# Block attention, then a mixture of experts: P·V of the split units in two passes, row sums on VectorE and GpSimd, Q loaded twice

## The chip, the cores and the metric

One core of a Trainium2 chip. The metric is the device time of one execution in microseconds; the kernel before takes 961.75 us, the median of 3 runs (961.17 to 962.17).

## The reference

Attention over 4 batches, 8 heads, 576 tokens, head size 64, with a mask by blocks of 64 (a query sees its own block of keys and all earlier ones), then four experts on all 2304 tokens, weighted by normalised probabilities. All in float32.

```python
scores = scale * np.matmul(q, k.transpose(0, 1, 3, 2))
scores = np.where(block_i >= block_j, scores, -1000000000.0)
scores = scores - np.max(scores, axis=-1, keepdims=True)
attn = np.exp(scores)
attn = attn / (np.sum(attn, axis=-1, keepdims=True) + 1e-09)
x = np.matmul(attn, v)          # then to 2304 x 512
...
for e in range(E):
    h = np.maximum(x @ w1[e], 0.0)
    out += p[:, e:e + 1] * (h @ w2[e])
```

## The kernel before, in words

**Tokens and blocks.** `BLOCKS` cuts the tokens into five: one of 256 (the first 64 tokens of each batch) and four of 512 (the other 512 of one batch each). For each block the experts run in 32 chunks (4 experts times 8 slices of 128 hidden units), 160 chunks in all. `mm1` (L915) makes h of a chunk by 12 products, `mm2` (L960) adds the chunk to the four accumulators in PSUM by 12 more (6 in the first block). Each float32 operand is split into a high and a low part in fp32r (`w1h`, `w1l`, `xh`, `xl`, `hh`, `hl`), and a product takes three passes: high by high, high by low, low by high. A weight slice comes in by DMA (`w1r`, `w2r`), is cast (`a_copy`, L319, on ScalarE or VectorE) and subtracted (`tt`, L326, on VectorE).

**Attention.** Attention for block p is computed while the experts work on block p-1, in units of two heads (`unit`): four units for each 512-token block, sixteen in all. The first four (batch 0, `plain`) multiply in float32. The other twelve are split units, done while blocks 1 to 3 (163 to 779 us) go through the experts: Q and K are split in high and low. K's two parts are stacked on the 128 partitions (`KK`), and Q stands on both halves (`HH` high, `LL` low), so that a score product takes two passes, HH and LL (L517, L518). `q_thread` loads Q to the lower 64 partitions and copies it to the upper ones by a second DMA (`qr<-qr`). The scores stand transposed: keys on partitions, queries along the free dimension, in five pieces of 512, 448, 320, 192 and 64 queries (`pieces_of`) in the tile `S`. GpSimd takes the maximum over keys with a reduction over all partitions (L612), VectorE subtracts it, ScalarE takes the exponential (L630, L637).

**P·V before.** `NARROW` = 192: pieces wider than 192 are split in `PH` and `PL`, the others go as float32 in `PJ`. `VS` holds V high beside ones, and V low beside zeros, for both heads; `VJ` holds V in float32 beside ones. `pv_flow` (L689) makes a head's output in one PSUM bank: PH by V high, PH by V low, PJ by V, PL by V high. The 64 columns of ones make the row sums in the other half of the bank. `sums` reads them out with 1e-9 added (L698), the outputs go to `xs`, and the sums are turned (L713), inverted, turned back and multiplied.

**What sets the order.** `Flow.run` is a planner: every operation is a thread's next step, with engine, cost, inputs and buffers; at each turn the operation that can start earliest on its engine is written out next (`est`). So a change of costs, of inputs or of a delay in `est` changes the order in which all engines' instructions stand. Each engine then works through its own queue in that order, and waits where an input is late. `est` also keeps GpSimd's work and VectorE's SBUF work apart (`port`). DMAs are issued by SyncE, in one queue.

Of the kernel before, what the change touches and what calls it, by code (L numbers as in the profile page):

```python
# [17 lines left out]
PEO = 13.5  # L18


NARROW = 192
# [13 lines left out]
STEPS = [(0, 0, 2), (1, 0, 2), (0, 2, 4), (1, 2, 4)]  # L35

# [21 lines left out]
class Op:  # L58
    __slots__ = ("eng", "cost", "fn", "r", "u", "prio", "val", "port", "pen", "bytes")

    def __init__(self, eng, cost, fn, r, u, prio):
        self.eng, self.cost, self.fn, self.r, self.u, self.prio = eng, cost, fn, r, u, prio
        self.val = Val()
        self.port = False
        self.bytes = 0
        self.pen = lambda: 0.0


class Flow:
# [34 lines left out]
    def est(self, op):  # L104
        best = None
        for eng, cost in (op.eng if isinstance(op.eng, list) else [(op.eng, op.cost)]):
            t = self.clock[eng]
            for v in op.r:
                if v.t is None:
                    return None  # L110
                x = v.t + (self.SELF if v.eng == eng else self.LAT + (self.SLACK if eng == "pe" else 0.0))
                if x > t:
                    t = x
            for b in op.u:
                if b.base + self.LAT > t:
                    t = b.base + self.LAT
# [87 lines left out]
def kernel(  # L204
# [40 lines left out]
    MAXN = max(pieces_of(j[1], j[2])[1] - sum(x) for j, x in zip(every, wide_of))  # L245
# [30 lines left out]
    bufs("PJ", 2, [P, MAXN])  # L276
# [31 lines left out]
    def op(eng, cost, fn, r=(), u=(), prio=0.0):  # L308
        p = prio if callable(prio) else (lambda: prio)
        return Op(eng, cost, fn, r, u, p)  # L310

# [51 lines left out]
    def unit(u, ua, us, ju, pu, ph, job, dst, c):  # L363
# [47 lines left out]
        def q_thread():  # L411
# [4 lines left out]
            for h in range(2):  # L416
                for j in range(2):
                    p0, c0 = (64 * h + 32 * j, 0) if plain else (32 * j, h * W)
                    vals.append((yield dma(
                        qr.tile[p0:p0 + 32, c0:c0 + W].rearrange("c (i r) -> c i r", r=32),  # L420
                        q[b, h0 + h, q0:q1, 32 * j:32 * j + 32].rearrange("(i c) r -> c i r", c=32),
                        W * 128, u=[qr], prio=pr)))
            if not plain:
                vals = [(yield dma(qr.tile[64:128, :2 * W], qr.tile[0:64, :2 * W], W * 512, vals, [qr], prio=pr))]
# [16 lines left out]
        def v_thread():  # L441
# [47 lines left out]
        def s_thread():  # L489
# [6 lines left out]
            KK, ka, kb = st["k"]  # L496
            if plain:
# [22 lines left out]
            for h, ps_list in banks:  # L520
# [4 lines left out]
                if h is None:  # L525
# [13 lines left out]
                    m = yield op("pe", 220.0, fn, need(None), use, pr)  # L539
# [3 lines left out]
                else:  # L543
                    at = 0
                    corners = []
                    for j, a, w, _ in ps_list:
# [4 lines left out]
                        m = yield op("pe", cost(w), fn, need(h), use, pr)  # L551
# [51 lines left out]
        def m_thread():  # L603
# [22 lines left out]
            def exp_head(h):  # L626
                PH = PL = PJ = a = l = e = None
                if wide:
                    e = yield op("act", 0.833 * ce + 95,
                                 lambda _: nc.scalar.activation(Sv[:, h, :ce], Sv[:, h, :ce], AF.Exp, scale=scale), subs, [Sb], pr)  # L630
                if plain:
                    j = yield op("act", 0.833 * C + 95, lambda _: nc.scalar.activation(
                        Sv[:, h, :C], Sv[:, h, :C], AF.Exp, scale=scale), subs, [Sb], pr)
                    PJ = Sb
                elif narrow:
                    PJ = yield fl.take("PJ", ju + h)
                    j = yield op("act", 0.833 * (C - ce) + 95, lambda _: nc.scalar.activation(  # L637
                        PJ.tile[:, :C - ce], Sv[:, h, ce:C], AF.Exp, scale=scale), subs, [Sb, PJ], pr)
                if wide:
                    PH = yield fl.take("PH", pu + h)  # L640
                    a = yield a_copy(PH.tile[:, :ce], Sv[:, h, :ce], ce, [e], [Sb, PH], pr)
                    PL = yield fl.take("PL", pu + h)
                    l = yield tt("dve", PL.tile[:, :ce], Sv[:, h, :ce], PH.tile[:, :ce], SUB, ce, [e, a], [Sb, PH, PL], pr)
                st["P"][h] = (PH, PL, a, l, PJ, j)

            for h in range(2):
                yield from exp_head(h)
            if not plain:
                fl.give(Sb)
# [16 lines left out]

    def pv_flow(st, q0, dst, c, W, wide, narrow, C, plain, pr, bank_tag):
# [5 lines left out]
        for h in range(2):  # L673
# [5 lines left out]
            for x, g, dep in ((PH, 0, a), (PH, 3, a), (PJ, None, pj), (PL, 0, l)):  # L679
                for j, _a, w, c0 in narrow if g is None else wide:  # L680
                    if g is not None:
                        lhsT, cost, dv, c1 = VS.tile[:, j, h + g:h + g + 2, :], w / 2.4 + PEO, vv, c0
                    else:
                        lhsT = VJ.tile[:, j - narrow[0][0], h:h + 2, :] if j is not None else VJ.tile[:, VJ.tile.shape[1] - 1, 1 - h:3 - h, :]
                        cost, dv, c1 = 2 * max(107.0, 2 * w / 2.4 + 2.5), jv, h * C + c0 if plain else c0 - narrow[0][3]
                    todo.append((lhsT, x.tile[:, c1:c1 + w], w, cost, dv + [dep]))
            for i, (lhsT, rhs, w, cost, dep) in enumerate(todo):
# [3 lines left out]
                m = yield op("pe", max(107.0, cost), fn, dep, [pb] + [x for x in (VS, VJ, PH, PL, PJ) if x], pr)  # L691
            if not plain:
                fl.give(*[x for x in (PH, PL, PJ) if x])
            hi, lo = slice(64 * h, 64 * h + 64), slice(64 - 64 * h, 128 - 64 * h)
# [10 lines left out]
        if plain:  # L705
# [382 lines left out]
```

## Time and profile before

| | |
|---|---|
| median of 3 runs | 961.75 us |
| profiled execution | 961.83 us |
| its span, first to last instruction | 959.7 us |
| granted TensorE clock, mean | 0.998 |
| TensorE, VectorE, ScalarE, GpSimd busy | 99%, 72%, 43%, 6% |
| instructions | 12822 |
| DMA | 107.84 MB, mean 112 GB/s |

The busy share of TensorE counts its matmuls' whole durations, and these overlap: a 512-column product lasts about 390 ns, but the next one starts some 227 ns later. What a product costs is therefore read from start to start. VectorE's instructions overlap a little too. The share in idle time of an engine that nothing waits for costs nothing.

### The profile page before, as it was taken

How to read it: one execution, taken by the hardware profiler on the slowest of the kernel's cores; microseconds unless marked ns; L12 is line 12 of the kernel's file. 1: busy time of each engine (PE TensorE's matmuls, PEld its weight loads, DVE VectorE, ACT ScalarE, POOL GpSimd, SP SyncE). 2: the span in 40 equal slices, each digit the busy share in tenths (PEclk: the TensorE clock that was granted, in tenths of full speed). 3: DMA queues.
4: the chain of work that ended last, by engine and by line, in shares of the span. 5: the costliest groups of instructions: out<-in, count | busy, mean ns of one | idle time of the engine just before them, and what ended most of it. 6: DMA issues, size and time to landing. Idle time of an engine off the chain costs nothing.

```text
span 959.7 us, 12822 instructions
## 1 busy us (share of the span) xinstructions
PE 949.4 (99%) x4454; PEld 778.6 (81%) x4454; DVE 692.6 (72%) x1267; ACT 411.2 (43%) x734; POOL 58.2 (6%) x39
## 2 busy tenths in 40 slices
PE   8999998999999999999999999999999999999998
PEld 4777787888888888888888888888888888888886
DVE  6788877899787768888687679887877454545452
ACT  3575654555454424644544245453544222222221
POOL 2111010100101001010101001101010000000000
PEclk9999999999999999999999999999999999999999
DMA  9754446544252353525253355333423343333321
GB/s 168 172 143 133 113 147 165 148 116 112 77 124 83 100 139 103 150 69 140 78 120 86 92 137 139 108 96 109 113 88 88 100 142 99 99 92 98 97 66 44
DMA packets 211648, 107.84 MB, mean 112 GB/s; under 512 B 106112, under 2 KB 188032, under 8 KB 211584
## 3 DMA queue, kind: packets, MB, share of 16 engines
q1 hardware_dynamic: 208416, 106.24, 41.6%
q10 hardware_dynamic: 3168, 0.79, 0.5%
q8 instruction: 35, 0.57, 0.3%
q14 instruction: 29, 0.24, 0.1%
HBM read 99.13 MB, written 4.72 MB: 108 GB/s over the span
## 4 chain that ended last, share of the span: by engine, by line
PE 91%; DVE 5%; issue 1%; SPq 1%; POOL 1%; DMA 0%; ACT 0%; DVEq 0%; POOLq 0%
PE h L915 39%; PE acc L960 38%; PE att L689 7%; PE att L518 2%; PE att L517 2%; PE acc L689 1%; PE acc L505 1%; PE att L505 1%; DVE o L989 1%; SPq L313 1%; DVE w2l L326 1%; DVE qT L428 1%; DVE LL L326 1%; DVE KK L326 0%; DMA qr<-qr 0%
## 5 line engine op out<-in xcount | busy, mean ns | idle before, releaser
L915 PE MATMUL h<-xh,w1h 128*128 128x512 f32 (+1 forms) x640 | 238.7, 373 | 0.0
L915 PE MATMUL h<-xh,w1l 128*128 128x512 f32 (+1 forms) x640 | 236.2, 369 | 0.0
L915 PE MATMUL h<-xl,w1h 128*128 128x512 f32 (+1 forms) x640 | 236.1, 369 | 0.0
L960 PE MATMUL acc<-w2h,hh 128*128 128x512 f32 x576 | 225.3, 391 | 0.0
L960 PE MATMUL acc<-w2l,hh 128*128 128x512 f32 x576 | 224.6, 390 | 0.0
L960 PE MATMUL acc<-w2h,hl 128*128 128x512 f32 x576 | 224.4, 390 | 0.0
L319 ACT CAST w2h<-w2r 128x512 fp32r<-128x512 f32 x157 | 97.7, 622 | 194.1 <-PE acc L960 184.5
L932 ACT ACTIVATE hh<-h 128x512 fp32r<-128x512 f32 (+1 forms) x160 | 89.0, 556 | 210.5 <-PE h L915 205.0
L326 DVE TENSOR_TENSOR w2l<-w2r,w2h 128x512 fp32r<-128x512 f32 x160 | 111.4, 696 | 92.5 <-ACT w2h L319 91.5
L915 PEld LDWEIGHTS h<-xh,w1h 128*128 128x128 f32 x640 | 120.8, 189 | 25.1 <-issue 5.5
L915 PEld LDWEIGHTS h<-xh,w1l 128*128 128x128 f32 x640 | 120.7, 189 | 20.4
L915 PEld LDWEIGHTS h<-xl,w1h 128*128 128x128 f32 x640 | 120.8, 189 | 19.6 <-DVE xl L326 0.2
L960 PEld LDWEIGHTS acc<-w2h,hl 128*128 128x128 f32 x576 | 108.1, 188 | 23.0 <-DVE hl L934 0.2
L960 PEld LDWEIGHTS acc<-w2h,hh 128*128 128x128 f32 x576 | 108.3, 188 | 21.9 <-issue 1.3
L960 PEld LDWEIGHTS acc<-w2l,hh 128*128 128x128 f32 x576 | 108.3, 188 | 20.4
L934 DVE SCALAR_TENSOR_TENSOR hl<-h,hh 128x512 fp32r<-128x512 f32 (+1 forms) x160 | 101.0, 631 | 28.3 <-ACT hh L932 28.0
L326 DVE TENSOR_TENSOR w1l<-w1r,w1h 128x512 fp32r<-128x512 f32 x160 | 110.2, 692 | 9.6 <-ACT w1h L319 3.7
L612 POOL PARTITION_ALL_REDUCE mx<-cm x16 | 52.7, 3292 | 657.4 <-DVE cm L326 470.1
L319 ACT COPY S<-att 128x512 f32<-128x512 f32 (+2 forms) x95 | 49.9, 525 | 56.2 <-DVE att L557 29.8
L319 DVE CAST w1h<-w1r 128x512 fp32r<-128x512 f32 x79 | 33.3, 422 | 48.9 <-PE h L915 48.3
L326 DVE TENSOR_TENSOR S<-S,mx 128x1024 f32<-128x1024 f32 (+4 forms) x80 | 59.9, 792 | 3.7 <-POOL mx L612 3.7
L319 ACT CAST w1h<-w1r 128x512 fp32r<-128x512 f32 x81 | 50.0, 617 | 10.3 <-DMA w1r<-in_moe_w_dram 10.2
(126 smaller groups left out, 820.9 us busy)
## 6 DMA issues: line engine op xcount, KB each, us to landing
w1r<-in_moe_w_dram SPq DMA_DIRECT2D x160, 256.0 KB, 2.9
w2r<-in_moe_w_dram SPq DMA_DIRECT2D x160, 256.0 KB, 2.8
kr<-in_k_dram SPq DMA_DIRECT2D x64, 72.0 KB, 3.0
qr<-in_q_dram SPq DMA_DIRECT2D x64, 64.0 KB, 2.4
out_dram<-o SPq DMA_DIRECT2D x16, 256.0 KB, 2.1
qr<-qr SPq DMA_DIRECT2D x12, 256.0 KB, 2.9
vr<-in_v_dram SPq DMA_DIRECT2D x24, 96.0 KB, 2.4
VN<-in_v_dram SPq DMA_DIRECT2D x8, 128.0 KB, 2.6
```

What stands on the lines that cost most here:

```text
L313: o = op(q, 550.0, lambda e: (nc.sync if e == "sp" else nc.scalar).dma_start(out=dst, in_=src), r, u, prio)
L319: o = op(engs, 0, lambda e: nc.scalar.copy(dst, src) if e == "act" else nc.vector.tensor_copy(dst, src), r, u, prio)
L326: o = op(engs, 0, lambda e: ENG[e].tensor_tensor(out=dst, in0=a, in1=b, op=alu), r, u, prio)
L505: nc.tensor.matmul(out=o, lhsT=KK.tile[hp, k0:k0 + n], rhs=qT.tile[hp, lo:W], start=True, stop=True)
L517: nc.tensor.matmul(out=o, lhsT=KK.tile[:, at:at + n], rhs=Hv[:, hs, lo:W], start=True, stop=False)
L518: nc.tensor.matmul(out=o, lhsT=KK.tile[:, at:at + n], rhs=Lv[:, hs, lo:W], start=False, stop=True)
L612: lambda _: nc.gpsimd.partition_all_reduce(mx.tile[:, :2 * W], src, P, RED.max),
L689: nc.tensor.matmul(out=o, lhsT=lhsT, rhs=rhs, start=(i == 0), stop=(i == n - 1))
L915: nc.tensor.matmul(out=ps[:, :n], lhsT=s.tile[:, ks], rhs=x.tile[:, kc, :n], start=(kc == 0 and m == 0), stop=(kc == KC - 1 and m == 2),)
L932: a = yield op("act", 0.833 * n + 55, lambda _: nc.scalar.activation(hh.tile[:, :n], ps[:, :n], AF.Relu), [mm], [pb, hh], 0.0)
L934: l = yield op("dve", 1.04 * n + 70, lambda _: nc.vector.scalar_tensor_tensor(out=hl.tile[:, :n], in0=ps[:, :n], scalar=0.0, in1=hh.tile[: ...
L960: nc.tensor.matmul(out=acc, lhsT=s.tile[:, ts], rhs=w.tile, start=(f == 0 and m == 0), stop=(f == FC - 1 and m == 2))
```

## The change

It has four parts.

1. `NARROW` becomes 64, so that the 192-wide piece is split too, and only the 64-wide one stays float32. `VS` holds, per tile and head, V high beside V low (for head 1 low beside high), without ones and zeros. PH and PL each make one pass over it: one half of the PSUM bank gets the part with V high, the other the part with V low, and the two halves are added on the way to `xs` (one copy to `rc`, one addition).
2. The row sums no longer come from the ones. VectorE adds the five pieces of the exponentials of both heads into the first (four additions per unit), and GpSimd sums over partitions, once per head. `S` is held until then. One exponential per head covers all pieces, `PJ` is gone.
3. Q is loaded from HBM to both halves: eight loads per unit in place of four and the copy.
4. `late` adds a delay in `est` for attention's products of split units: 1500 ns for the score products, half of that for P·V.

```diff
-NARROW = 192
+NARROW = 64
...
+LAG = 1500.0
...
-                x = v.t + (self.SELF if v.eng == eng else self.LAT + (self.SLACK if eng == "pe" else 0.0))
+                x = v.t + (self.SELF if v.eng == eng else self.LAT + op.lag + (self.SLACK if eng == "pe" else 0.0))
...
-                if b.base + self.LAT > t:
-                    t = b.base + self.LAT
+                if b.base + self.LAT + op.lag / 2 > t:
+                    t = b.base + self.LAT + op.lag / 2
...
-    bufs("VS", 2, [P, MAXT, 6, D], F32R)
+    bufs("VS", 2, [P, MAXT, 4, D], F32R)
...
-            if not plain:
-                vals = [(yield dma(qr.tile[64:128, :2 * W], qr.tile[0:64, :2 * W], W * 512, vals, [qr], prio=pr))]
+            for h, j in ((h, j) for h in range(2) for j in range(2 if plain else 4)):
+                p0, c0 = (64 * h + 32 * j, 0) if plain else (32 * j, h * W)
+                vals.append((yield dma(
+                    qr.tile[p0:p0 + 32, c0:c0 + W].rearrange("c (i r) -> c i r", r=32),
+                    q[b, h0 + h, q0:q1, 32 * (j % 2):32 * (j % 2) + 32].rearrange("(i c) r -> c i r", c=32),
+                    W * 128, u=[qr], prio=pr)))
...
-                a = yield a_copy(vs[:, :, 0:3:2, :], vr.tile[:, :n], n * 128, vals, [vr, VS], pr + 0.005)
-                l = yield tt(BOTH, vs[:, :, 3:6:2, :], vr.tile[:, :n], vs[:, :, 0:3:2, :], SUB, n * 128, [a], [vr, VS],
+                a = yield a_copy(vs[:, :, 0:4:3, :], vr.tile[:, :n], n * 128, vals, [vr, VS], pr + 0.005)
+                l = yield tt(BOTH, vs[:, :, 1:3, :], vr.tile[:, :n], vs[:, :, 0:4:3, :], SUB, n * 128, [a], [vr, VS],
                              pr + 0.005)
...
-                        m = yield op("pe", cost(w), fn, need(h), use, pr)
+                        m = yield late(op("pe", cost(w), fn, need(h), use, pr), lag)
...
+            got = [x for h in range(2) for x in st["P"][h][2:4] + st["P"][h][5:]]
+            for _, a, w, c0 in pcs[1:]:
+                acc = Sv[:, :, a - q0:W]
+                got = [(yield tt("dve", acc, acc, Sv[:, :, c0:c0 + w], ADD, 2 * w, got, [Sb], pr))]
+            st["sums"] = []
+            for h in range(2):
+                st["sums"].append((yield op("pool", 150 + 6.3 * W, lambda _, h=h: nc.gpsimd.partition_all_reduce(
+                    Sv[:, h, W:2 * W], Sv[:, h, :W], P, RED.add), got, [Sb], pr)))
...
-            for x, g, dep in ((PH, 0, a), (PH, 3, a), (PJ, None, pj), (PL, 0, l)):
-                for j, _a, w, c0 in narrow if g is None else wide:
-                    if g is not None:
-                        lhsT, cost, dv, c1 = VS.tile[:, j, h + g:h + g + 2, :], w / 2.4 + PEO, vv, c0
+            for x, split, dep in ((PH, True, a), (PJ, False, pj), (PL, True, l)):
+                for j, _a, w, c0 in wide if split else narrow:
+                    if split:
+                        lhsT, cost, dv, c1 = VS.tile[:, j, 2 * h:2 * h + 2, :], w / 2.4 + PEO, vv, c0
...
+                x = yield a_copy(rc.tile[hi, :W], ps[lo, :W], W, [m], [pb, rc], pr, True)
+                parts.append((yield tt("dve", xs.tile[hi, :W], ps[hi, :W], rc.tile[hi, :W], ADD, W, [m, x], [pb, rc, xs], pr)))
...
+            for h, s in enumerate(st["sums"]):
+                hi = slice(64 * h, 64 * h + 64)
+                got = yield op("dve", 1.04 * W + 70, lambda _, h=h, hi=hi: nc.vector.transpose(
+                    out=t1[hi], in_=PJ.tile[hi, h * C + W:h * C + 2 * W]), [s], [PJ, tr], pr)
```

Three places show how the order moves. The first is TensorE's queue at one head's P·V products of the first split unit, before:

```order
L689 MATMUL att_130<-PH_118,VS_103 128x512
L689 MATMUL att_130<-PH_118,VS_103 128x448
L689 MATMUL att_130<-PH_118,VS_103 128x320
L689 MATMUL att_130<-PH_118,VS_103 128x512
L689 MATMUL att_130<-PH_118,VS_103 128x448
L689 MATMUL att_130<-PH_118,VS_103 128x320
L689 MATMUL att_130<-PJ_110,VJ_105 128x192
L689 MATMUL att_130<-PJ_110,VJ_105 128x64
L689 MATMUL att_130<-PL_116,VS_103 128x512
L689 MATMUL att_130<-PL_116,VS_103 128x448
L689 MATMUL att_130<-PL_116,VS_103 128x320
```

and with the change:

```order
L696 MATMUL att_128<-PH_116,VS_103 128x512
L696 MATMUL att_128<-PH_116,VS_103 128x448
L696 MATMUL att_128<-PH_116,VS_103 128x320
L696 MATMUL att_128<-PH_116,VS_103 128x192
L696 MATMUL att_128<-S_111,VJ_105 128x64
L696 MATMUL att_128<-PL_114,VS_103 128x512
L696 MATMUL att_128<-PL_114,VS_103 128x448
L696 MATMUL att_128<-PL_114,VS_103 128x320
L696 MATMUL att_128<-PL_114,VS_103 128x192
```

Three fp32r products and one fp32 product go, two fp32r products of 192 columns come (an fp32 product shows as two in the trace).

The second is TensorE's queue where the first 512-token block begins (the first three rows are the last accumulations of the block before), before:

```order
L960 MATMUL acc_126<-w2h_71,hh_81 128x512
L960 MATMUL acc_126<-w2l_75,hh_81 128x512
L960 MATMUL acc_126<-w2h_71,hl_83 128x512
L517 MATMUL att_130<-HH_101,KK_99 128x512
L518 MATMUL att_130<-LL_102,KK_99 128x512
L517 MATMUL att_129<-HH_101,KK_99 128x448
L518 MATMUL att_129<-LL_102,KK_99 128x448
L915 MATMUL h_123<-xh_90,w1h_61 128x512
L915 MATMUL h_123<-xl_92,w1h_61 128x512
L915 MATMUL h_123<-xh_90,w1l_65 128x512
```

and with the change:

```order
L979 MATMUL acc_124<-w2h_71,hl_83 128x512
L934 MATMUL h_121<-xh_90,w1h_61 128x512
L934 MATMUL h_121<-xl_92,w1h_61 128x512
L934 MATMUL h_121<-xh_90,w1l_65 128x512
L934 MATMUL h_121<-xh_90,w1h_61 128x512
L934 MATMUL h_121<-xl_92,w1h_61 128x512
L934 MATMUL h_121<-xh_90,w1l_65 128x512
L522 MATMUL att_128<-HH_101,KK_99 128x512
L523 MATMUL att_128<-LL_102,KK_99 128x512
L522 MATMUL att_127<-HH_101,KK_99 128x448
L523 MATMUL att_127<-LL_102,KK_99 128x448
```

Six h products of the block's first chunk now stand ahead of the first score products. SyncE's queue for the same unit, before:

```order
L313 DMA kr_93<-in_k_dram 32x18x32 x4
L313 DMA qr_95<-in_q_dram 32x16x32 x4
L313 DMA vr_96<-in_v_dram 128x3x64 x2
L313 DMA VJ_105<-in_v_dram 64x64
L313 DMA VJ_105<-in_v_dram 128x64
L313 DMA VJ_105<-in_v_dram 64x64
L313 DMA qr_95<-qr_95 64x1024
L313 DMA VJ_105<-in_v_dram 128x64
L313 DMA w1r_77<-in_moe_w_dram 128x4x128
L313 DMA w2r_79<-in_moe_w_dram 128x512
```

and with the change:

```order
L320 DMA kr_93<-in_k_dram 32x18x32 x4
L320 DMA qr_95<-in_q_dram 32x16x32 x8
L320 DMA vr_96<-in_v_dram 128x4x64 x2
L320 DMA VJ_105<-in_v_dram 64x64
L320 DMA w1r_77<-in_moe_w_dram 128x4x128
L320 DMA w2r_79<-in_moe_w_dram 128x512
L320 DMA VJ_105<-in_v_dram 64x64
```

Between K's loads and the weights of the block's first chunk (`w1r_77`) there stood four Q loads, two loads of `vr`, four of `VJ` and the copy; now there stand eight Q loads, two of `vr` and one of `VJ`.

The third is VectorE's queue after the first split unit's PL subtractions, with the change (`S` the exponentials, `tr` the turned sums; the transpose waits for GpSimd's sum):

```order
L333 TENSOR_TENSOR S_111<-S_111 128x2x192
L333 TENSOR_TENSOR LL_102<-qT_98,HH_101 128x1024
L333 TENSOR_TENSOR S_111<-S_111 128x2x64
L333 TENSOR_TENSOR w1l_65<-w1r_77,w1h_61 128x512
L333 TENSOR_TENSOR w2l_73<-w2r_79,w2h_69 128x512
L333 TENSOR_TENSOR xs_119<-att_128,rc_120 64x512
L326 COPY cm_117<-att_127 128x64
L562 MEMSET att_128 64x64
L729 STREAM_TRANSPOSE tr_109<-S_111 64x512
L953 SCALAR_TENSOR_TENSOR hl_84<-h_122,hh_82 128x512
```

Before, none of the additions into `S` stood there, nor the additions to `xs`, and the transpose read the sums that TensorE had made. Over the whole program 40 casts of `w1h` move from VectorE's queue to ScalarE's (79 and 81 before, 39 and 121 now).

## Rows read from the trace of the kernel before

**Rows 1.** The page: the chain that ended last, shares of the span.

```profile
PE 91%; DVE 5%; issue 1%; SPq 1%; POOL 1%; DMA 0%; ACT 0%; DVEq 0%; POOLq 0%
```

**Rows 2.** Busy time by stretch: blocks 1, 2, 3; columns in the first line.

```profile
core 0: us, PE busy (x) PEld busy (x) DVE busy (x) ACT busy (x) POOL busy (x), PEclk, DMA share, GB/s
163.30:371.10 207.80, 207.47 (x953) 174.07 (x952) 164.93 (x300) 98.19 (x174) 12.99 (x4) 0.99 0.43 113
371.10:576.60 205.50, 205.17 (x948) 172.04 (x946) 163.06 (x287) 92.94 (x162) 12.89 (x4) 1.00 0.42 109
576.60:779.00 202.40, 202.07 (x928) 169.26 (x927) 153.53 (x265) 88.29 (x151) 12.89 (x4) 1.00 0.38 104
```

**Rows 3.** Timeline of TensorE, one head's P·V: start us, length us, instruction.

```profile
193.59 1.33 PE L689 MATMUL att<-PH,VS 128*128 128x512 f32 x6
194.76 0.65 PE L689 MATMUL att<-PJ,VJ 128*128 128x192 f32 x4
195.22 0.82 PE L689 MATMUL att<-PL,VS 128*128 128x512 f32 x3
195.89 0.39 PE L915 MATMUL h<-xh,w1h 128*128 128x512 f32 x1
```

**Rows 4.** Timeline of TensorE: two 192-column score products and what follows.

```profile
211.01 0.25 PE L517 MATMUL att<-HH,KK 128*128 128x192 f32 x1
...
211.21 0.41 PE L915 MATMUL h<-xh,w1h 128*128 128x512 f32 x1
```

**Rows 5.** Timeline at block 1's entry; last, a stretch with the columns of rows 2.

```profile
149.30 2.09 SPq L313 DMA_DIRECT2D qr<-in_q_dram  x4
...
154.54 0.53 SPq L313 DMA_DIRECT2D qr<-qr  x1
...
160.47 0.62 ACT L319 CAST w1h<-w1r 128x512 fp32r<-128x512 f32 x1 [2.07 <-DMA w1r<-in_moe_w_dram]
...
161.29 0.49 PE L517 MATMUL att<-HH,KK 128*128 128x512 f32 x1 [1.99 <-DVE HH L319]
...
162.41 0.68 DVE L326 TENSOR_TENSOR w1l<-w1r,w1h 128x512 fp32r<-128x512 f32 x1
162.55 0.50 PE L518 MATMUL att<-LL,KK 128*128 128x512 f32 x1 [0.77 <-DVE LL L326]
...
163.30 0.54 PE L915 MATMUL h<-xh,w1h 128*128 128x512 f32 x1
...
163.30:166.80 3.50, 3.50 (x12) 2.91 (x11) 2.68 (x8) 1.43 (x3) 0.00 (x0) 0.51 0.53 173
```

**Rows 6.** Timeline of TensorE: two score products of 512 columns at 290 us.

```profile
289.78 0.39 PE L517 MATMUL att<-HH,KK 128*128 128x512 f32 x1
...
290.83 0.37 PE L517 MATMUL att<-HH,KK 128*128 128x448 f32 x1
```

**Rows 7.** Groups by shape: count, busy us, mean ns, idle before.

```profile
L326 DVE TENSOR_TENSOR S<-S,mx 128x896 f32<-128x896 f32 x16 | 17.4, 1085 | 0.0
L326 DVE TENSOR_TENSOR S<-S,mx 128x128 f32<-128x128 f32 x16 | 4.6, 286 | 0.0
L326 DVE TENSOR_TENSOR PL<-S,PH 128x1280 fp32r<-128x1280 f32 x24 | 35.7, 1487 | 3.5 <-ACT PH L319 3.4
L713 DVE STREAM_TRANSPOSE tr<-rc 128x512 f32<-128x512 f32 x16 | 11.4, 710 | 5.1 <-ACT rc L698 5.0
L319 DVE CAST w1h<-w1r 128x512 fp32r<-128x512 f32 x79 | 33.3, 422 | 48.9 <-PE h L915 48.3
```

**Rows 8.** Timeline: two of GpSimd's reductions, and a VectorE subtraction inside each.

```profile
179.91 3.22 POOL L612 PARTITION_ALL_REDUCE mx<-cm  x1 [57.33 <-DVE cm L326]
...
180.81 1.54 DVE L326 TENSOR_TENSOR w1l<-w1r,w1h 128x512 fp32r<-128x512 f32 x1
...
302.15 3.22 POOL L612 PARTITION_ALL_REDUCE mx<-cm  x1 [43.17 <-DVE cm L326]
...
304.50 0.69 DVE L326 TENSOR_TENSOR w2l<-w2r,w2h 128x512 fp32r<-128x512 f32 x1 [1.85 <-ACT w2h L319]
```

More of the change, by code (lines that the diff above doesn't have):

```diff
@@ L58 @@
 class Op:
-    __slots__ = ("eng", "cost", "fn", "r", "u", "prio", "val", "port", "pen", "bytes")
+    __slots__ = ("eng", "cost", "fn", "r", "u", "prio", "val", "port", "pen", "bytes", "lag")
     def __init__(self, eng, cost, fn, r, u, prio):
@@ L65, in __init__ @@
         self.bytes = 0
+        self.lag = 0.0
         self.pen = lambda: 0.0
@@ L310, in op, with late @@
         return Op(eng, cost, fn, r, u, p)
+    def late(o, by):
+        o.lag = by
+        return o
     def dma(dst, src, nbytes, r=(), u=(), prio=0.0, q="sp"):
@@ L496, in s_thread @@
             KK, ka, kb = st["k"]
+            lag = 0.0 if plain else LAG
             if plain:
@@ L626, in exp_head @@
             def exp_head(h):
[L627 to L638, printed above, removed]
+                PH = PL = a = l = None
@@ L644, in exp_head @@
-                st["P"][h] = (PH, PL, a, l, PJ, j)
+                    a = yield a_copy(PH.tile[:, :ce], Sv[:, h, :ce], ce, [j], [Sb, PH], pr)
+                    l = yield tt("dve", PL.tile[:, :ce], Sv[:, h, :ce], PH.tile[:, :ce], SUB, ce, [j, a], [Sb, PH, PL], pr)
+                st["P"][h] = (PH, PL, a, l, Sb, j)
             for h in range(2):
                 yield from exp_head(h)
-            if not plain:
-                fl.give(Sb)
+            if plain:
+                return
+            got = [x for h in range(2) for x in st["P"][h][2:4] + st["P"][h][5:]]
@@ L712, in pv_flow @@
         t1, t2 = tr.tile[:, :W], tc_.tile[:, :n]
-        got = yield op("dve", 1.04 * W + 70, lambda _: nc.vector.transpose(out=t1, in_=rt[:, :W]), sums, [rc, tr], pr)
-        got = yield op("dve", 6.25 * n + 70, lambda _: nc.vector.reciprocal(
-            out=t2, in_=t1.rearrange("p (i c) -> p i c", c=32)[:, :, 0]), [got], [tr, tc_], pr)
+        t0 = t1.rearrange("p (i c) -> p i c", c=32)[:, :, 0]
+        if plain:
+            got = yield op("dve", 1.04 * W + 70, lambda _: nc.vector.transpose(out=t1, in_=rt[:, :W]), sums, [rc, tr], pr)
+        else:
+            yield ("until", lambda: len(st.get("sums", ())) == 2)
+            for h, s in enumerate(st["sums"]):
+                hi = slice(64 * h, 64 * h + 64)
+                got = yield op("dve", 1.04 * W + 70, lambda _, h=h, hi=hi: nc.vector.transpose(
+                    out=t1[hi], in_=PJ.tile[hi, h * C + W:h * C + 2 * W]), [s], [PJ, tr], pr)
+            fl.give(PJ)
+            got = yield op("dve", 80.0, lambda _: nc.vector.tensor_scalar_add(t2, t0, 1e-9), [got], [tr, tc_], pr)
+            t0 = t2
+        got = yield op("dve", 6.25 * n + 70, lambda _: nc.vector.reciprocal(out=t2, in_=t0), [got], [tr, tc_], pr)
         got = [(yield op("dve", 1.04 * W + 70, lambda _: nc.vector.transpose(
@@ L1038 @@
         identity()
-        nc.scalar.copy(fl.free["PJ"][0].tile[:, :1], nc.const_aps.tensor(1.0, [P, 1], F32))
+        nc.scalar.copy(fl.free["rc"][0].tile[:, 32:33], nc.const_aps.tensor(1.0, [P, 1], F32))
         for _ in range(WARM):
```

46 lines of the change are left out of this document (16 added, 30 removed).

## The prediction

> **What bounds the kernel now.** I read the chain of waits first, then the busy time by stage, then single stretches of the timeline. The chain that ended last is TensorE for 91% of the span and VectorE for 5% [rows 1]. By stage, the three 512-token blocks that carry attention last 207.80, 205.50 and 202.40 us, 615.7 together, and in each TensorE is busy for all but 0.33 us, while VectorE is busy 164.93, 163.06 and 153.53 us, 481.5 together or 78% [rows 2]. So here a microsecond of matmuls removed is a microsecond of the kernel, as long as what the matmuls read is not late; VectorE has 134 us of room, and nothing before 130 us or after 779 us is touched except by a shift. TensorE's few waits are two: the one at the entry to the first of these blocks [rows 5], and a small one once in each block [rows 6]. All sums stand against the profiled execution: 961.83 us, 2.1 us of it outside the span of 959.7; the median of the runs is 961.75, the same to 0.1 us.
>
> **PV products (24 heads).** A head's products run from 193.59 to 195.89 us, 2.30 us, with nothing between them [rows 3]: six PH products (three tiles, against two sets of weights) in 1.17 us, the two fp32 pieces of 192 and 64 columns in 0.46, three PL products in 0.67. The change leaves one PH pass over three tiles, half of 1.17 or 0.585; the fp32 piece of 64 columns; the PL pass, 0.67; and two new 192-column products. Two 192-column products of the same number type run in 0.20 us together [rows 4], so 0.10 each. The 64-column piece is at least a quarter of the 0.46 by its columns, 0.115, and at most half, 0.23; I take 0.14, near the column share, since the longer piece must take most. That is 0.585 + 0.14 + 0.67 + 0.20 = 1.60, so 0.70 less per head and **16.8 us** for 24 heads (14.6 with 0.23, 17.4 with 0.115).
>
> **The entry to the first block.** TensorE waits 1.99 us for HH and 0.77 for LL, 2.76 together, and for the next 3.5 us its granted clock is 0.51, the lower of its two levels, which costs another 1.7 us [rows 5]. The change places six h products ahead of those score products and loads Q directly, without the copy from half to half. That looks like a cure, but the six h products need the first weights of this block, and these are late too: ScalarE waited 2.07 us for their transfer, cast them at 160.47 (0.62 us), VectorE subtracted at 162.41 (0.68), and h started at 163.30, 0.21 us after [rows 5]. In the new order of SyncE's queue that transfer stands behind four more Q loads (2.09 us for four) and ahead of one V load, without the copy (0.53) and without two V loads, which I take to issue in about that time too [rows 5]: 2.09 less 1.6, about 0.5 us later, unless a transfer of 128-byte runs lands slower than the copy did. With VectorE free earlier (LL no longer waits for the copy) the weights are ready at about 160.5 + 0.5 + 0.62 + 0.68 = 162.3, against TensorE's arrival at 159.3. So the wait is 3.0 instead of 2.76 and the low clock stays: **0 us**. The ends: all of it goes, -4.5; or the new loads cost the whole 2.1 again, +2.
>
> **The score products placed later.** In each block one unit's HH product started before LL was there: 289.78 to 290.83, 1.05 us for two products of 1024 columns together [rows 6], which take 0.47 at the pace of the PH products, 1.17 us for 2560 columns [rows 3]; 0.58 lost, the same in each of the three blocks, 1.8 us. The planner now leaves 1.5 us more before a score product, more than the 1.05, so I book **-1.8**. Moving products later costs nothing by itself, since h and acc products stand in their place.
>
> **VectorE and GpSimd.** Per unit (12 of them) VectorE gains four additions whose shapes are those of the subtractions of the maximum, 1085 ns for the first and 286 for the last of four evenly spaced ones, 2.74 us together; two additions of 512 columns that read PSUM, booked like the 512-wide transpose, 710 each; one more such transpose, 710; and 192 more columns in two PL subtractions, 1487 x 192/1280 = 223 each [rows 7]. 2.74 + 1.42 + 0.71 + 0.45 = 5.32, times 12 is 64 us. The order moves 40 casts of w1h to ScalarE, 40 x 422 ns = 16.9 us less [rows 7], so VectorE rises by 47 us, to 528.5 in three stages that shrink to 615.7 - 16.8 = 598.9: 88% busy. ScalarE is under half busy [rows 2] and takes the casts in its idle time. If that cover is gone, the subtraction behind each cast is late next, then an h product.
>
> GpSimd gains 24 sums over partitions. The trace has only the maximum, 3.22 us for 1024 columns [rows 8]; a sum of 512 is bounded by half of that and, from above, by the planner's own 3.4 us in the diff. I take the upper end. Its result is needed only by the normalisation, far ahead of the next block, so the duration itself is off the path. What it does to VectorE is not. A subtraction with both inputs in SBUF that began 0.90 us into a maximum took 1.54 instead of 0.69 us: it was held until 1.75 us into it [rows 8]. Another, begun 2.35 us into one, took 0.69 though the maximum still ran. So a reduction shuts out such work for about its first 1.75 us. 36 of them would cost VectorE 63 us if it had nothing else to do in them: 528.5 + 63 = 591.5, still under 598.9, but without room. As it runs h's subtraction and other PSUM reads meanwhile, I book only **+1.0** for new waits, about half of what the old order left on TensorE by LL.
>
> Three edits go together at nothing: one exponential per head in place of two, the S tile held until its sums are read (there are two, and four units to a block of 200 us), and the fill of VS with constants that is gone. VJ's zero fill takes the place of its ones.
>
> Sum: 961.8 - 16.8 + 0 - 1.8 + 1.0 = 944.2; I say **944.0**.
>
> **Rivals.** *All of TensorE's old waits go*, the weights too: 961.8 - 16.8 - 1.8 - 4.5 = 938.7. For it: the weights' transfer is not held by the copy any more; against: the same queue holds four more loads. Chance 0.13.
>
> *VectorE is late in part.* If each of the 24 added reductions makes TensorE wait 0.3 us, as LL did, about 7 us come back: 951. For it: no room in 591.5 against 598.9, and in the new order the subtractions for w1l and w2l stand right behind the additions that start the sums. Chance 0.2.
>
> *VectorE becomes the bound: slower.* The place is the same three stages. VectorE needs 528.5 + 36t, with t the time that one reduction shuts it out, against 615.7 before: from t = 2.42 us the kernel is slower. With t the whole 3.22 us it is 644.4, 28.7 more, 990. Against it: t was 1.75, and 36 waits in full would need every reduction to meet such work. For it: no sum is in the trace, and a transpose that waits for one holds all of VectorE's queue behind it, h's subtraction included. Chance 0.04. The Trainium skill, "SBUF — State Buffer", section "SBUF: two separate sides", says that a DVE operation with two SBUF inputs and a GpSimd operation share a port pair under an exclusive lock for the full instruction; by that rule the time is the 990 of this rival. The trace agrees that there is a lock and disagrees on its length, as the 0.69 us subtraction inside a running maximum shows.
>
> *The change doesn't shorten what ends last.* If TensorE, done sooner with PV, only waits longer for hl or the weights, the time stays at about 961. Against it: in the stages it waits for neither now. Chance 0.03.
>
> **How the numbers follow.** The forecast has the remaining 0.6, with its own range 941 to 947 by the ends of the 64-column piece and of the new waits. The range runs from the first rival, 938.5, to just past the second, 952; left out are the slower case, the unchanged one, and some of the tails. Two runs of this kernel are told apart from about 0.2%, 1.9 us: every case but the last two is faster, so 0.93 faster, 0.03 within, 0.04 slower.
>
> **What would show it.** In the profile after: a head's PV products last 1.60 us; L517's successor no longer waits for LL inside the blocks; at the first block's entry TensorE waits 2 to 3 us for w1l, followed by some 3.5 us at the lower clock; the three stages together last about 598 us with TensorE busy for all but a few; VectorE is busy 84 to 90% of them. The sum over partitions takes up to 3.4 us and stretches a subtraction here and there. I am wrong if TensorE waits for hl, w1l or w2l inside the blocks for more than 5 us together, or if the PV products of a head take over 1.8 us.

## The result: 946.64 us, and the profile after

The changed kernel takes 946.64 us (945.34 to 947.18, four runs) against 961.46 (961.17 to 962.17, four runs) for the kernel before in the same job: a ratio of 0.9843, 95% interval 0.9827 to 0.9859. It is faster by 15 us, and 2.6 us slower than the forecast of 944.0, within the range given. The profiled execution took 946.28 us with a span of 944.5. Lines of code move: the score products of `L517` and `L518` are now `L522` and `L523`, P·V is `L696`, the additions and subtractions of two tensors `L333`, the casts `L326`, `h` `L934`, the `acc` products `L979`, the sums over partitions `L653`.

The page of the changed kernel: the chain that ended last and GpSimd's two groups (count, busy us, mean ns, idle before).

```profile
PE 91%; DVE 3%; DMA 2%; SPq 2%; issue 1%; ACT 1%; DVEq 0%; ACTq 0%
...
L653 POOL PARTITION_ALL_REDUCE S<-S x24 | 81.1, 3428 | 256.2 <-DVE S L333 234.5
L617 POOL PARTITION_ALL_REDUCE mx<-cm x16 | 55.2, 3451 | 349.4 <-DVE cm L333 235.2
```

Against [rows 1] TensorE keeps its 91% of the chain. The 24 sums take 3.43 us each on average, as the planner's own figure of 3.4 had it.

Busy time by stage in the changed kernel, blocks 1 to 3 (columns in the first line):

```profile
core 0: us, PE busy (x) PEld busy (x) DVE busy (x) ACT busy (x) POOL busy (x), PEclk, DMA share, GB/s
161.30:362.40 201.10, 199.64 (x918) 166.61 (x919) 177.73 (x308) 101.75 (x169) 41.57 (x12) 1.00 0.45 117
362.40:564.20 201.80, 200.94 (x928) 167.87 (x927) 179.53 (x308) 100.92 (x166) 40.19 (x12) 1.00 0.43 113
564.20:763.50 199.30, 197.88 (x911) 165.29 (x910) 169.39 (x290) 93.14 (x150) 40.68 (x12) 1.00 0.41 108
sum 602.20, PE 598.47 PEld 499.76 DVE 526.65 ACT 295.81 POOL 122.44; mean PE 199.49 PEld 166.59 DVE 175.55 ACT 98.60 POOL 40.81
```

The three stages last 602.20 us where they lasted 615.7 [rows 2]: 13.5 less, and 4.1 above the 598.1 that the forecast's terms leave there (615.7 - 16.8 - 1.8 + 1.0). Of the 4.1, some 0.9 is a matter of where the stage begins: the block's first four score products stand ahead of 163.30 in the kernel before [rows 5] and behind 161.30 here. VectorE is busy 526.65 us of them, 87%. And TensorE, which lacked 0.33 us per stage before, now lacks 1.46, 0.86 and 1.42.

TensorE in the changed kernel, one head's P·V (start us, length us, instruction, how many):

```profile
244.98 0.84 PE L696 MATMUL att<-PH,VS 128*128 128x512 f32 x4
245.66 0.35 PE L696 MATMUL att<-S,VJ 128*128 128x64 f32 x2
245.82 0.92 PE L696 MATMUL att<-PL,VS 128*128 128x512 f32 x4
246.58 0.42 PE L979 MATMUL acc<-w2h,hh 128*128 128x512 f32 x1
246.83 0.40 PE L979 MATMUL acc<-w2l,hh 128*128 128x512 f32 x1
247.07 0.39 PE L979 MATMUL acc<-w2h,hl 128*128 128x512 f32 x1
247.30 0.40 PE L979 MATMUL acc<-w2h,hh 128*128 128x512 f32 x1
```

From 244.98 to 246.58 is 1.60 us, against 2.30 in [rows 3]. The `acc` products behind it start 0.25, 0.24 and 0.23 us apart.

What TensorE waited for from 160 to 765 us of the changed kernel (who waited, for whom: total us, times, longest):

```profile
PE att L522 <- DVE xs L333: 2.6, 2, 1.4
PE h L934 <- ACT w1h L326: 1.7, 1, 1.7
PE att L522 <- DVE cm L333: 0.9, 1, 0.9
PE h L934 <- DVE w1l L333: 0.3, 1, 0.3
```

The two `h` waits are the entry to block 1. The other three, 3.5 us together, are new: score products that wait for VectorE to read a PSUM bank empty, `xs` and `cm` being what it reads it into. No product waits for LL any more. One of the three, on the timeline of VectorE and its neighbours in the changed kernel:

```profile
292.47 1.22 DVE L333 TENSOR_TENSOR LL<-qT,HH 128x1024 fp32r<-128x1024 f32 x1
...
292.72 7.31 POOL L653 PARTITION_ALL_REDUCE S<-S  x2 [25.02 <-DVE S L333]
...
293.60 2.73 DVE L333 TENSOR_TENSOR w1l<-w1r,w1h 128x512 fp32r<-128x512 f32 x1
...
296.26 0.68 DVE L333 TENSOR_TENSOR w2l<-w2r,w2h 128x512 fp32r<-128x512 f32 x1
...
296.97 0.69 DVE L333 TENSOR_TENSOR xs<-att,rc 64x512 f32<-64x512 f32 x1
...
297.72 0.47 PE L522 MATMUL att<-HH,KK 128*128 128x448 f32 x1 [1.21 <-DVE xs L333]
```

The subtraction for w1l, 0.68 us by itself, takes 2.73 while the sum runs. The subtraction for w2l and the addition to `xs` stand behind it in VectorE's queue; that addition is the last reader of a PSUM bank, and TensorE's next score product needs the bank. So on this reading what hurts is not that a result is late: the sum holds a subtraction, and the queue behind it holds TensorE. VectorE does wait for the sums' results too, at five of the transposes:

```profile
DVE tr L729 <- POOL S L653: 5.4, 5, 2.7
```

Which of the two costs TensorE its 3.5 us is for the runs to show.

### The profile page after: what moved, and what is told of

Read it like the earlier page. It is cut to its first block, busy times and chain, and to the rows that moved or that the text cites. A ratio compares the mean times of both kernels' runs of the same rounds, so it can differ in the third digit from the quotient of the medians.

```text
span 944.5 us, 12695 instructions
## 1 busy us (share of the span) xinstructions
PE 930.7 (99%) x4381; PEld 761.2 (81%) x4382; DVE 736.5 (78%) x1319; ACT 426.5 (45%) x730; POOL 141.1 (15%) x59
## 4 chain that ended last, share of the span: by engine, by line
PE 91%; DVE 3%; DMA 2%; SPq 2%; issue 1%; ACT 1%; DVEq 0%; ACTq 0%
PE h L934 40%; PE acc L979 40%; PE att L696 5%; SPq L320 2%; PE att L522 2%; PE att L523 2%; PE acc L696 1%; DMA w2r<-in_moe_w_dram 1%; DVE w1l L333 1%; PE acc L510 1%; PE att L510 1%; DMA S<-in_v_dram 1%; DVE w2l L333 0%; DMA S<-in_k_dram 0%; DVE hl L953 0%
## 5 line engine op out<-in xcount | busy, mean ns | idle before, releaser
L934 PE MATMUL h<-xh,w1h 128*128 128x512 f32 (+1 forms) x640 | 238.3, 372 | 1.7 <-ACT w1h L326 1.7
L934 PE MATMUL h<-xh,w1l 128*128 128x512 f32 (+1 forms) x640 | 235.7, 368 | 0.3 <-DVE w1l L333 0.3
L934 PE MATMUL h<-xl,w1h 128*128 128x512 f32 (+1 forms) x640 | 235.7, 368 | 0.1
L979 PE MATMUL acc<-w2h,hh 128*128 128x512 f32 x576 | 227.1, 394 | 0.1
L979 PE MATMUL acc<-w2h,hl 128*128 128x512 f32 x576 | 224.6, 390 | 0.3 <-DVE hl L953 0.3
L979 PE MATMUL acc<-w2l,hh 128*128 128x512 f32 x576 | 224.7, 390 | 0.0
L326 ACT CAST w2h<-w2r 128x512 fp32r<-128x512 f32 x153 | 95.2, 622 | 164.6 <-PE acc L979 156.9
L333 DVE TENSOR_TENSOR w2l<-w2r,w2h 128x512 fp32r<-128x512 f32 x160 | 114.4, 715 | 60.3 <-ACT w2h L326 59.9
L934 PEld LDWEIGHTS h<-xh,w1h 128*128 128x128 f32 x640 | 120.5, 188 | 27.4 <-issue 5.5
L934 PEld LDWEIGHTS h<-xh,w1l 128*128 128x128 f32 x640 | 120.4, 188 | 20.9 <-DVE w1l L333 0.7
L934 PEld LDWEIGHTS h<-xl,w1h 128*128 128x128 f32 x640 | 120.6, 188 | 20.0 <-DVE xl L333 0.3
L979 PEld LDWEIGHTS acc<-w2h,hl 128*128 128x128 f32 x576 | 108.1, 188 | 24.4 <-DVE hl L953 1.2
L333 DVE TENSOR_TENSOR w1l<-w1r,w1h 128x512 fp32r<-128x512 f32 x160 | 119.5, 747 | 9.7 <-ACT w1h L326 6.1
L979 PEld LDWEIGHTS acc<-w2h,hh 128*128 128x128 f32 x576 | 108.3, 188 | 21.4 <-issue 1.3
L979 PEld LDWEIGHTS acc<-w2l,hh 128*128 128x128 f32 x576 | 108.4, 188 | 19.5
L653 POOL PARTITION_ALL_REDUCE S<-S x24 | 81.1, 3428 | 256.2 <-DVE S L333 234.5
L617 POOL PARTITION_ALL_REDUCE mx<-cm x16 | 55.2, 3451 | 349.4 <-DVE cm L333 235.2
L326 ACT CAST w1h<-w1r 128x512 fp32r<-128x512 f32 x121 | 74.5, 617 | 18.5 <-DMA w1r<-in_moe_w_dram 18.2
L326 ACT COPY S<-att 128x512 f32<-128x512 f32 (+2 forms) x91 | 47.8, 526 | 53.7 <-DVE att L562 34.2
L333 DVE TENSOR_TENSOR S<-S,mx 128x1024 f32<-128x1024 f32 (+4 forms) x80 | 60.0, 792 | 3.3 <-POOL mx L617 3.3
```

The lines of the kernel that those rows point to most:

```text
L326: o = op(engs, 0, lambda e: nc.scalar.copy(dst, src) if e == "act" else nc.vector.tensor_copy(dst, src), r, u, prio)
L333: o = op(engs, 0, lambda e: ENG[e].tensor_tensor(out=dst, in0=a, in1=b, op=alu), r, u, prio)
L617: lambda _: nc.gpsimd.partition_all_reduce(mx.tile[:, :2 * W], src, P, RED.max),
L653: st["sums"].append((yield op("pool", 150 + 6.3 * W, lambda _, h=h: nc.gpsimd.partition_all_reduce(Sv[:, h, W:2 * W], Sv[:, h, :W], P, RED ...
L934: nc.tensor.matmul(out=ps[:, :n], lhsT=s.tile[:, ks], rhs=x.tile[:, kc, :n], start=(kc == 0 and m == 0), stop=(kc == KC - 1 and m == 2),)
L979: nc.tensor.matmul(out=acc, lhsT=s.tile[:, ts], rhs=w.tile, start=(f == 0 and m == 0), stop=(f == FC - 1 and m == 2))
```

## The experiments

Twelve runs followed, each timed against the kernel before. My theory after the first look: the sums over partitions shut VectorE out of work with two SBUF inputs, and the three new waits are what comes of it. The rivals: the waits come from the sums' *results*, from the later placing, or from the Q loads.

### The change once more, without the sums, and with sums that nobody reads

The change itself ran again as a control.

> The change once more, on the chip of the next three, as their yardstick. Lock theory: GpSimd's new sums hold back VectorE's subtractions of two SBUF inputs; behind one of these stands what frees a PSUM bank, and TensorE's first score product of a unit waits for the bank: 1.4, 1.0 and 1.6 us at three places (296, 408 and 653 us of the span), at the same three places again, 946.6 us within 1. If these waits are chance, they stand elsewhere in this profile.

945.90 us, ratio 0.9845 (0.9832 to 0.9858), with the same waits at the same three places (297.29, 408.67 and 654.64 us): 2.6 for `xs` and 0.8 for `cm`. At the entry it waited 0.7 and 1.0. In what follows, "control" is this run.

The sums taken out of GpSimd's queue, nothing else moved:

```diff
-    lambda _, h=h: nc.gpsimd.partition_all_reduce(Sv[:, h, W:2 * W], Sv[:, h, :W], P, RED.add)
+    lambda _, h=h: None
```

> The change with the 24 sums over partitions left out on GpSimd (so the output lacks them); the order of all other queues is the same row by row. Lock theory: no subtraction is stretched after 180 us except at the 12 maxima, the three waits are gone, 4 us less than the change, 942 to 943. Rival, the chain that frees the bank (a copy on ScalarE, then an addition on VectorE) is too long by itself: the waits stay, same time as the change. If the sums cost nothing at all (my booked +1): 1 us less.

942.59 us, 0.9808 (0.9795 to 0.9822), 3.3 less than the control. VectorE's and ScalarE's instructions stand in the same order as in the change, one by one. What TensorE waited for there from 155 to 780 us:

```profile
PE h L934 <- ACT w1h L326: 1.1, 1, 1.1
PE h L934 <- DVE w1l L333: 1.0, 1, 1.0
```

Only the entry is left. Around the same place w1l takes its usual time:

```profile
293.60 1.22 DVE L333 TENSOR_TENSOR LL<-qT,HH 128x1024 fp32r<-128x1024 f32 x1
...
294.74 0.69 DVE L333 TENSOR_TENSOR w1l<-w1r,w1h 128x512 fp32r<-128x512 f32 x1
```

The sums made, but over their own input, so that their old place is what the normalisation reads and no instruction reads a sum:

```diff
-    partition_all_reduce(Sv[:, h, W:2 * W], Sv[:, h, :W], P, RED.add)
+    partition_all_reduce(Sv[:, h, :W], Sv[:, h, :W], P, RED.add)
```

> The change with the sums made as before but written over their own input, so that nothing reads them (the transposes read other data, the output lacks the sums); all queues have the same rows. It tells the lock from waiting for the result. Lock theory: the same three waits, same time as the change within 0.5 us. Rival, VectorE stands still at the transpose that waits for a sum: the waits go, 942 to 943 as without the sums.

946.44 us, 0.9851 (0.9836 to 0.9866): the time of the change. TensorE's waits from 155 to 780 us:

```profile
PE att L522 <- DVE xs L333: 2.5, 2, 1.3
PE h L934 <- DVE w1l L333: 1.0, 1, 1.0
PE h L934 <- ACT w1h L326: 1.0, 1, 1.0
PE att L522 <- DVE cm L333: 0.9, 1, 0.9
```

The transposes no longer wait for a sum here (the row with 5.4 us is gone), and w1l still takes 2.73 us, at 293.02. So a sum costs by running, not by being waited for. The three bank waits, and 3.3 us, belong to the sums.

### The bank emptied by copies

The bank is read by two plain copies and given back; the addition runs afterwards from SBUF, where it may be late.

```diff
-  parts.append((yield tt("dve", xs.tile[hi, :W], ps[hi, :W], rc.tile[hi, :W], ADD, ...
+  y = yield a_copy(xs.tile[hi, :W], ps[hi, :W], W, [m], [pb, xs], pr, True)
   fl.give(pb)
+  parts.append((yield tt("dve", xs.tile[hi, :W], xs.tile[hi, :W], rc.tile[hi, :W], ADD, ...
```

> The change, but a head's PSUM bank is emptied by two plain copies (on ScalarE, or VectorE) and the addition is made afterwards from SBUF, so that the bank no longer depends on an addition that stands behind a held subtraction. Lock theory, with the bank as the link: the two waits for the addition (1.4 and 1.6 us) go, the one for the maximum (1.0) may stay; 943 to 944 us. If VectorE's load rather than the bank's release is the link: no gain, 946 or more, since the addition from SBUF can be held too.

944.60 us, 0.9818 (0.9787 to 0.9850), 1.3 less than the control, just above the 943 to 944 expected, and with an interval that overlaps the control's. The waits for `xs` and `cm` are gone, which fits the chain but does not prove its last link: the planner also placed the score products elsewhere (the 512-wide one that stood at 295.21 in the change comes at 306.95), so nothing wanted the bank at the old places. A new wait came: `h` waits 0.8 us for `xl` (the low half of `x`) at the entry to block 2.

### The moves alone, and undone within the change

The Q loads and the later placing, put into the kernel before with its old P·V:

> The kernel before with only Q loaded twice and attention's products placed later (LAG 1500), without the two-pass P.V and the new sums. My terms: the three waits for LL go (-1.8), the entry to the first block stays as it is or loses up to 4.5: 957 to 960 us. Rival, that most of the change's gain comes from the placing: 950 or less. If placing later makes waits of its own: 961 or more.

957.80 us, 0.9964 (0.9951 to 0.9978): 3.7 less than the kernel before of that job, with 1.3 us of waits, all at the entry, and none for LL. Q loaded twice alone, in the kernel before:

> The kernel before with only Q loaded twice, without the later placing. With both moves it took 957.8, 3.7 less than before. If that gain is the placing's (LL waits 1.8 and the entry): 961 to 962 here. If the direct loads make it: 958 to 959.

959.15 us over twelve runs, 0.9973 (0.9964 to 0.9982): 2.6 less. The wait for HH at the entry is gone, and the one for LL is 0.76 us. TensorE in that kernel:

```profile
158.68 0.39 PE L514 MATMUL att<-HH,KK 128*128 128x512 f32 x1
...
159.82 0.50 PE L515 MATMUL att<-LL,KK 128*128 128x512 f32 x1 [0.76 <-DVE LL L326]
```

HH and LL are earlier, as the copy that came after Q's loads, and that both waited for, is no longer there; the granted clock stays at 1.00 behind this wait. Inside the blocks one wait for LL is left, 0.16 us, where there were three of 0.33: loading Q twice does by itself most of what the prediction credited to the later placing. Whether the placing adds to it in the kernel before is not clear, since the two intervals overlap. Then each move undone within the change. No later placing:

```diff
-LAG = 1500.0
+LAG = 0.0
```

> The change with LAG 0, attention's products placed as the old rule has them. My term: the waits for LL come back (+1.8), and the bank waits grow, as the first score products stand up to 1.5 us earlier: 948 to 953. Rival, that the placing is worth nothing here since other work stands in the place of the wait: 946 to 947.

942.16 us, 0.9796 (0.9766 to 0.9827). A miss: I expected LL waits and a longer time, and it is 3.7 us shorter than the control. At the entry there are waits of 0.2 for HH and 1.5 for LL, inside the blocks 0.2 for a bank and none for LL, although nothing is placed later. Q loaded once and copied, as before the change:

```diff
-  for h, j in ((h, j) for h in range(2) for j in range(2 if plain else 4)):
+  for h, j in ((h, j) for h in range(2) for j in range(2)):
...
+  if not plain:
+      vals = [(yield dma(qr.tile[64:128, :2 * W], qr.tile[0:64, :2 * W], W * 512, vals, [qr], prio=pr))]
```

> The change with Q loaded once and copied to the upper half, as before. My term for loading Q twice was 0 (between -4.5 and +2). If it is 0, the same 946 within 1.5 us; the order differs, so the bank waits may stand elsewhere. If the direct loads are what shortened the entry (its wait fell from 2.8 to some 2.3 us and the low clock is mostly gone): 948 to 949.

940.72 us (940.24 to 941.80), 0.9785 (0.9766 to 0.9804). A miss as well, and the fastest kernel of this study, 5.2 us under the control. TensorE's waits from 160 to 765 us:

```profile
PE h L936 <- DVE w1l L333: 1.0, 1, 1.0
PE att L524 <- DVE cm L333: 0.2, 1, 0.2
```

The sums still hold subtractions here (w1l takes 2.33 us at 492.57 and 2.10 at 736.07), but only the first stands ahead of a bank that TensorE wants, by way of `w2l` and a transpose, and it costs the 0.2 us above. At the entry the planner put the first weights of block 1 earlier: their cast starts at 157.80, against 160.58 in the change. So the two moves, which together gain in the kernel before, each lose within the change. As far as the waits tell, it is not by what they do themselves: TensorE waited 5.1 us in the control, 1.9 without later placing and 1.2 here, and that is most of both differences. Each edit makes the planner lay the whole order anew, and in some orders a bank's last reader stands behind a held subtraction.

### The weights first, and edits together

The transfers of the weights of the chunk after next ranked ahead of attention's loads:

```diff
-  else (2.5 if i <= now[0] + 2 else 5.0)
+  else (1.9 if i <= now[0] + 2 else 5.0)
```

> The change with the weights of the chunk after next put ahead of attention's loads in the planner's priorities (1.9 in place of 2.5), so that the first 512-token block's weights no longer queue behind the eight Q loads. My reading of the entry: its wait for w1h and w1l (about 2.3 us in the change) goes, 944 to 945 us if nothing else moves. Rival, Q comes later and the wait returns at the score products: same time as the change.

942.90 us, 0.9802 (0.9771 to 0.9833). The entry has no wait left, as expected; four bank waits for `cm`, 2.8 us, are. Each ends 4 to 5 us after the start of a held w1l (2.43, 2.65, 2.45 and 2.42 us long, from 209.23, 254.57, 401.22 and 446.15), which stands ahead of that `cm` in VectorE's queue: the same chain at other places. With the copies as well:

> Both, the bank emptied by two copies and the weights first. If the two causes are separate, their gains add: 941 to 942.5 us, the fastest so far that computes all. If one shifts the order so that the other's wait returns elsewhere: 943 to 946.

943.16 us, 0.9805 (0.9775 to 0.9836): the gains do not add. Without later placing and with the weights first:

> The change with LAG 0 and the weights first. LAG 0 alone gave 942.2 and left a wait of 2.1 us for LL at the entry; the weights first alone gave 942.9 and left four bank waits. If the two gains are separate, 939 to 941. If LL is late again at the entry, since Q now queues behind weights: 942 to 944.

944.31 us, 0.9822 (0.9802 to 0.9841), a miss: one bank wait of 1.93 us behind w1l, which took 2.73 us at 686.03, and then 3.5 us at the lower clock. Busy time by stretch there, columns as above:

```profile
684.00:690.00 6.00, 4.07 (x19) 3.10 (x18) 5.61 (x7) 2.31 (x4) 4.86 (x2) 0.98 0.03 11
690.00:693.50 3.50, 3.50 (x12) 3.00 (x11) 1.40 (x5) 0.89 (x2) 2.41 (x1) 0.55 0.25 68
693.50:697.00 3.50, 3.50 (x17) 2.89 (x16) 2.54 (x6) 1.94 (x5) 0.00 (x0) 1.00 0.00 0
```

12 products in the 3.5 us at 0.55, 17 in the next 3.5: the one wait cost 1.9 and then some 1.6 more. All three edits together:

> The same with the bank emptied by two copies. If a bank that waits for VectorE's addition is still a cost at LAG 0: 1 to 2 us less than the one with LAG 0 and the weights first. If not, the same, within 1 us: the two copies are then work that frees nothing.

945.19 us, 0.9830 (0.9811 to 0.9849), 0.9 more than without the copies. By the number that is "the same, within 1 us", but not for the reason given there. Timeline at 396 us:

```profile
396.65 6.45 POOL L653 PARTITION_ALL_REDUCE S<-S  x2 [20.93 <-ACT w1h L326]
...
396.75 3.22 DVE L333 TENSOR_TENSOR LL<-qT,HH 128x1024 fp32r<-128x1024 f32 x1
...
400.03 0.50 PE L523 MATMUL att<-LL,KK 128*128 128x512 f32 x1 [1.66 <-DVE LL L333]
```

The bank is free, but here it is LL itself that starts 0.10 us into a sum, and takes 3.22 instead of 1.22 us. It happens twice, 3.7 us of waits.

### All versions side by side

Each version's median, and what TensorE waited from 155 to 780 us of its profiled execution.

| version | median us | waits of TensorE, us | profiled time less these waits |
|---|---|---|---|
| before | 961.46 | 3.8, then low clock | 958.0 |
| before, Q twice | 959.15 | 0.9 | 957.6 |
| before, both moves | 957.80 | 1.3 | 957.7 |
| change | 946.64 | 5.5 | 940.8 |
| change again | 945.90 | 5.1 | 940.5 |
| sums unread | 946.44 | 5.4 | 940.2 |
| all three edits | 945.19 | 4.1 | 942.2 |
| bank emptied by copies | 944.60 | 2.9 | 942.3 |
| LAG 0, weights first | 944.31 | 2.1, then low clock | 943.6 |
| copies, weights first | 943.16 | 1.2 | 941.6 |
| weights first | 942.90 | 2.8 | 940.8 |
| sums left out | 942.59 | 2.1, then low clock | 941.0 |
| LAG 0 | 942.16 | 1.9 | 940.2 |
| Q copied | 940.72 | 1.2 | 939.5 |

In the last column the kernels fall into two groups: 957.6 to 958.0 with the old P·V, and 939.5 to 943.6 with the new one. The matmuls removed make the difference between the groups, some 16 us. Among the new ones the profiled times lie within 5.5 us, and with the waits taken away still within 4.1. So the waits, which hang on where the planner puts things, explain the pairs compared above, but not every difference: the lower clock is one more part (1.6 us at 690 us above), when TensorE ends block 0 another (from 158.3 to 160.1 us), and the rest stays open.

## Why the prediction held, and what was mis-sized

**PV products (16.8 booked).** A head takes 1.60 us, as worked out. Start to start, the P·V products of the three stages sum to 37.5 us where they took 55.0, 17.5 less; the `acc` products, which now often stand behind a narrow product (64 to 192 columns), sum to 1.8 us more. That leaves 15.7. The missing 1.1 are those first `acc` products behind a narrow one, which I had taken at their usual 0.23 us.

**The entry (0 booked, ends -4.5 and +2).** The waits came as the prediction put them, first for the weights' cast and then for the subtraction: 1.7 and 0.3 us against the 3.0 worked out. Start to start the entry's waits cost 3.2 us before and 2.3 now, so 0.9 was won. The step that failed is "the low clock stays": the granted clock in the windows behind the entry is 1.00, where it was 0.51 in [rows 5], and by their spacing the products there had lost 1.6 us (I had worked out 1.7). Both control and change show this; the version without sums, with waits of 1.1 and 1.0 at the same place, shows 0.51 for the 3.5 us behind them. The order of the instructions does not settle it: the mean granted clock of a whole execution differs among executions of one kernel. It runs from 0.997 to 1.000 in the eight of the change (945.97, 947.18 and 947.46 us at 0.997, 945.34 and 945.82 at 1.000), and 3.5 us at half the clock would take some 0.002 off that mean, an estimate from the span of 944.5. So the clock's part is a gain of the two executions compared, not of every one. Why it falls in one and not in the other stays open.

**LL (1.8 booked).** No product inside the blocks waits for LL in the change. Start to start the three waits had cost 1.5 us, and all of it is gone. The number is near, but its reason is not the one I gave: without later placing none of these waits comes back, with Q copied as before none does either, and in the kernel before, Q loaded twice leaves one of 0.16. Either move was enough.

**New waits (1.0 booked, 4.0 measured).** This is the term that was mis-sized. Start to start the three bank waits cost 4.0 us. My estimate had two faults. The sum's lock is longer than the maximum's: LL that began 0.10 us into one was held 2.0 us (3.22 against 1.22), so the sum shuts such work out for about 2.1 of its 3.2 us, where I carried over 1.75 from the maximum [rows 8]. And I asked for VectorE's room as a whole, 591.5 of 598.9 us, when what matters is which instruction stands behind the held one. The trace of before had a row for that, w1l held to 1.54 us in [rows 8]; nothing followed it there that TensorE was about to need.

The Trainium skill, "SBUF — State Buffer", section "SBUF: two separate sides", says that whichever of a DVE op with two SBUF inputs and a GpSimd op starts first has the shared port pair for its whole instruction. That the lock excludes both ways agrees with the trace: the pair of sums that began at 292.72, with LL still running, took 7.31 us, against 6.45 for the pair at 396.65, which began ahead of LL. On the length it does not agree: by that rule the LL which began 0.10 us into a sum would have needed 3.1 + 1.2 = 4.3 us, and it took 3.22.

**VectorE (528.5 booked, 526.65 measured).** The two agree by luck. The 528.5 was the sum by shapes, with nothing held by the sums; the same instructions without GpSimd's sums keep VectorE busy for 515.96 us (160.08 to 760.43 us there), so the shapes were booked 12.5 too high, and the holding adds some 11. For the holding I had 63 us in 36 reductions. Twelve of the weights' subtractions run over 1 us in the change, 13 us of stretch in all, and two in the version without sums, 2 us; TensorE noticed three. The rival in which VectorE becomes the bound needed t = 2.42 us in all 36 reductions; t is about 2.1 for a sum that meets such work all along, and the 24 sums together added those 11 us. The rival in which VectorE is late in part, 951, had the mechanism right but not its spread: 3.3 us, the control against the version without sums, at three places, instead of 0.3 at each of the 24.

**What is left.** The profiled executions differ by 15.55 us (961.83 less 946.28). PV 15.7, LL 1.5, the clock 1.6 and the entry's waits 0.9, less 4.0 of bank waits and 0.3 in block 0, make 15.4; the remaining 0.2 is not assigned. The start-up is no part of it: the first `h` product of block 0 starts between 22.0 and 24.2 us in the executions of all these kernels, 23.9 in the one before and 22.2 in the one after, but the lead is gone when block 0 ends, where the last `acc` product starts at 158.91 before and at 159.16 after.

So the sum, 944.2, came within 2.1 us of the profiled execution partly by luck. It was too low by 3.0 for the new waits, 1.1 for P·V, 0.3 for LL and 0.3 for block 0; the clock and the entry's waits, booked at nothing, gave 2.5 of that back.

## What to carry to other kernels

When a change gives GpSimd reductions to a kernel whose VectorE is nearly full, do not price them by the sum of busy times: look in VectorE's queue for each subtraction or addition with both inputs in SBUF that will meet one, and for what stands right behind it, the release of a PSUM bank above all. Where a planner lays the order, an edit also buys another order: here kernels with the same products came out between 940.7 and 946.6 us, so an effect of under about 6 us is not the edit's own until the waits in the trace say so. The edit that takes one such wait away can bring another, as three of these versions did (the copies, the weights first, and all three edits).

## What the runs showed of the hardware beyond what was expected

- A sum over partitions of 128x512 takes 3.2 us when nothing holds it, no less than a maximum of 1024 columns at 3.22 [rows 8]. I had half of that as the lower bound.
- The sum excludes VectorE's work with two SBUF inputs for about 2.1 us from its start, the maximum for about 1.75. A subtraction that reads one of its inputs from PSUM runs meanwhile: hl takes its usual 0.69 us at 293.90, inside a sum that began at 293.21, in the version with copies, and the w1l after it took 2.01 (that pair began with an addition of two SBUF inputs still running, and took 7.00 us for 6.45, so by an estimate its own start is some 0.55 later):

```profile
293.21 7.00 POOL L653 PARTITION_ALL_REDUCE S<-S  x2 [23.88 <-DVE S L333]
...
293.90 0.69 DVE L954 SCALAR_TENSOR_TENSOR hl<-h,hh 128x512 fp32r<-128x512 f32 x1
294.51 2.01 DVE L333 TENSOR_TENSOR w1l<-w1r,w1h 128x512 fp32r<-128x512 f32 x1
```

- A wait of TensorE can cost nearly twice its length, as at 690 us in the version without later placing and with the weights first: 1.93 us, then 3.5 at 0.55. Other waits of 1.4 and 1.7 us, in the change, had 1.00 behind them.
